# Where fourteen weight loads stand among attention's slots: from slot 3 to 26 instead of from 1 to 26

## The chip, the cores and the metric

The kernel runs on one core of a Trainium2 chip. The metric is the device time of one execution in microseconds (us). The runs are unprofiled; beside them stands one execution that the hardware profiler recorded, from which all views of the profile come. Engines in the text: PE (TensorE matmuls; PEld its weight loads), DVE (VectorE), ACT (ScalarE), POOL (GpSimd), SP (SyncE, which only issues DMAs here).

## The reference: what is computed

Blockwise causal attention, whose result is the input of a mixture-of-experts layer with one expert a token:

- `q`, `k`, `v` are 8 batches x 8 heads x 576 tokens x 64 in float32. Scores are `q k^T / 8`, masked so that a block of 64 tokens sees itself and the blocks before it, then a softmax and the product with `v`.
- The result is laid out as `x`, 8 x 576 rows of 512. `logits = x w_gate` (8 experts), `local_gate = sigmoid(x w_local)`. A token takes its own best expert if it is the first of its batch or its local gate is under 0.5, otherwise the expert of the token before it.
- Each token's output is `p[e] * (relu(x w1[e]) w2[e])`, with `w1` 8 x 512 x 1024 and `w2` 8 x 1024 x 512, and `p` the softmax of the logits.

## The kernel before

**Attention in 32 slots.** A slot is one pair of heads of one batch (`NPAIR = 32`, four slots a batch); the loop is `for i in range(NPAIR)` at line 1045, with `r = i % 4`. The order of instructions on each engine is written out by hand (`tc.manual_schedule()`). Slot `i` does, in this order:

1. `load_qk(i + 2)` (line 787): SP issues the loads of k and q of the pair after next, 256 KB each in 1 KB pieces (line 797), and two small ones (line 802). They go into one staging area, so k of pair `i + 2` can only be issued when POOL has copied k of pair `i + 1` out of it.
2. `behind(i)` (line 1037): `values(i - 1)` on PE (line 920), the additions of the softmax sums on DVE (line 932), and `load_v(i + 1)` on SP (line 813): two v loads of 128 KB in 256-byte pieces (line 819), one a head, and a small one. There are two v buffers, so v of pair `i + 1` is issued when `values(i - 1)` is done with its buffer, and it is read by `values(i + 1)` in slot `i + 2`. In slot 1 alone (`swap`) `behind` comes after the scores.
3. The scores of pair `i` on PE (line 882), their exponentials on ACT (line 892), and POOL's clearing of masked corners (line 869), for which `values(i)` waits.
4. `transposes(i + 1)`: PE transposes k and q of the next pair (line 844), ACT copies them out of PSUM (line 839).
5. `tasks(i)`: for r = 0 and 2 the sums and gates of half a batch (line 696); for r = 1 logits and two tiles of rows of `x` of the batch before; for r = 3 its other three tiles. Each tile of rows is stored to HBM by SP (line 668, 128 KB, the last one 64 KB). In the first batch slots 1 and 3 have no tasks. Beside that, short steps of the routing run on DVE; in slot 4 they make constants on POOL (lines 222 to 246).
6. `arrange(i + 2)` (line 805): POOL copies k and q of the pair after next into the order that the transposes need (line 810, two copies).
7. At the end of some slots, `load_weights` (line 105): POOL issues one DMA that reads 2 MB of float32 weights and writes 1 MB of bf16. Even loads are a `w1` (line 107), odd ones a `w2` (line 111). Which slots these are is what the change touches.

The last two weight loads do not go by that formula: `w1` of expert 7 follows the routing's first half, `w2` of expert 7 stands at slot 30, since their space is scratch and staging until then.

**The experts.** After attention 38 tiles of up to 128 tokens are gathered by expert, multiplied by `w1` (line 994) and `w2` (line 1128) on PE, and scattered to the output (line 1135). Nothing there is touched.

**Queues.** All DMAs issued by SP share one queue on each of the chip's DMA engines (q1 in the profile), all issued by POOL another one (q0). SP issues in order and waits before an issue when the DMA eight issues earlier has not landed.

Of the kernel before, what the change touches and what calls it, by code (L numbers as in the profile page):

```python
# [62 lines left out]
def kernel(  # L63
# [23 lines left out]
    E = moe_w_gate.shape[1]  # L87
# [125 lines left out]
    def row_of_x(x):  # L213
        return x[:, :XH].bitcast(BF16)
# [551 lines left out]
    with tc.tile_pool(name="atn_const", bufs=1) as cst, \  # L766
# [13 lines left out]
        def constants():  # L780
            nc.vector.memset(sel, 0.0)
            nc.vector.memset(sel[:, 16 + E + 1:16 + E + 2], 1.0)
            nc.vector.memset(L[64:, :, :], 0.0)
# [3 lines left out]
        def load_qk(i):  # L787
            if i >= NPAIR:
                return
            b, p = divmod(i, HP)  # L790
            h2 = slice(2 * p, 2 * p + 2)
            tl = ld.tile([P, 2, D], F32, tag="qkl", name="qkl")
            raws[i] = [tl]
            for j, src in enumerate((k, q)):

                m = staged[:, j].rearrange("p (h j d) -> p h j d", h=2, j=4)
                nc.sync.dma_start(
                    out=m.rearrange("p h j d -> p h (j d)"),
                    in_=src[b, h2, :512].rearrange("h (p j) d -> p h (j d)", j=4))
                raws[i].append(m)  # L800
            for j, src in enumerate((k, q)):
                nc.sync.dma_start(out=tl[64 * j:64 * j + 64],
                                  in_=src[b, h2, 512:].rearrange("h s d -> s h d"))

        def arrange(i, copies):
            if i >= NPAIR:
                return
            for j in range(2):
                m = staged[:, 2 + j].rearrange("p (j h d) -> p j h d", j=4, h=2)
                copies[j](m, raws[i][1 + j].rearrange("p h j d -> p j h d"))  # L810
                raws[i][1 + j] = m
# [41 lines left out]
        def transposes(i, copy):  # L853
            if i >= NPAIR:
                return
            ps = psp.tile([P, 2, 512], F32, tag="sc", name="kq")
            for part in range(2):
                turn_part(i, part, ps[:, part])
            back_in_order(i, slice(0, 2), ps, copy)
            turn_tail(i)  # L860
# [10 lines left out]
        def scores(i, u):  # L871
            if i >= NPAIR:
                return
            if u == 0:
                Ss[i] = Sb[i % NSB]
            t = qkTs[i % 2]
            ps = psp.tile([P, 2, 512], F32, tag="sc", name="sc")
            col = 0
            for c, q0, n in UNITS[u]:
                for h in range(2):  # L880
                    r = slice(64 * h, 64 * h + 64)
                    nc.tensor.matmul(ps[:, h, col:col + n], lhsT=t[r, 0, c * P:c * P + P],  # L882
                                     rhs=t[r, 1, q0:q0 + n], start=True, stop=True)
                col += n
            return ps

        def exps(i, u, ps):
            if i >= NPAIR:
                return
            for col, n, c, q0 in EXPS[u]:  # L890
                rows = slice(0, CW[c])
                nc.scalar.activation(exps_at(i, c, q0, n, rows), ps[rows, :, col:col + n],  # L892
                                     func=AF.Exp, scale=scale_attn)
            for c, q0, n in UNITS[u]:
                if q0 == c * P and c < 4:
                    clear(i, c)

        def last_scores(i):
            if i >= NPAIR:
                return  # L900
            t = qkTs[i % 2]
            for h in range(2):
                r = slice(64 * h, 64 * h + 64)

                nc.tensor.matmul(po[:, LAST[h]:LAST[h] + ST],
                                 lhsT=t.rearrange("p a s -> p (a s)")[r, 512:512 + P],
                                 rhs=t[r, 1, 512:], start=True, stop=True)
            for h in range(2):
                nc.scalar.activation(Pc[i % 2][:ST, h, POS[4]:],
                                     po[:ST, LAST[h]:LAST[h] + ST],  # L910
                                     func=AF.Exp, scale=scale_attn)
# [14 lines left out]
        def add_chunks(i):  # L926
            if not 0 <= i < NPAIR:
                return
            for c in range(1, NC):
                n = S - P * c  # L930
                rows = slice(0, CW[c])
                nc.vector.tensor_add(Ss[i][rows, :, P * c:], Ss[i][rows, :, P * c:],  # L932
                                     Pc[i % 2][rows, :, POS[c]:POS[c] + n])
# [44 lines left out]
        def weights_at(w, ev):  # L978
            nc.vector.tensor_copy(w, w1_bf[:, bass.ds(ev, WE)])  # L979
            return w  # L980
# [21 lines left out]
        def expert(ph, j, engines=(mybir.EngineType.PE, mybir.EngineType.DVE)):  # L1002
            return nc.values_load(
                et_i[ph][0:1, j:j + 1], engines=engines, min_val=0,
                max_val=(E - 1) * WE,
                skip_runtime_bounds_check_because="the table is clamped to the last expert")

        def bf(x, n):
            return x.rearrange("p a s -> p (a s)").bitcast(BF16)[:, :n]
# [25 lines left out]
        wload = 0  # L1035

        def behind(i):

            values(i - 1)
            if not swap:  # L1040
                add_chunks(i - 1)
            load_v(i + 1)
            steps.vector(1.4)

        for i in range(NPAIR):
            slot[0] = i
            load_qk(i + 2)


            swap = i == 1  # L1050
            if not swap:
                behind(i)
            if i == NPAIR - 1:

                tiles = [(0, j) for j in range(NS[0])] + [(1, j) for j in range(NS[1])]
                ev = {j: expert(*tiles[j]) for j in range(2)}
                w = weights_at(bf(Pc[0], WE), ev[0])

                free = bf(Sb[(NPAIR - 3) % NSB], 2 * S * 2)[:, -AHEAD * Dm:]
                xTs = {}  # L1060
                for j in range(AHEAD):
                    xTs[j] = free[:, j * Dm:(j + 1) * Dm].rearrange("p (k n) -> p k n", k=KO1)
                    nc.sync.dma_start(out=xTs[j], in_=row_of_x(xgs[j]), transpose=True)
            for u in range(len(UNITS)):
                exps(i, u, scores(i, u))
                if u == 0:
                    last_scores(i)
                    if i == 0:
                        transposes(1, nc.vector.tensor_copy)
                        constants()  # L1070
                        for h in range(2):
                            hs = slice(64 * h, 64 * h + 64)
                            nc.sync.dma_start(
                                out=wg2[hs, :, 16 * h:16 * h + E],
                                in_=moe_w_gate.rearrange("(p h d) e -> h d p e", h=2, d=D)[h])
                            nc.sync.dma_start(
                                out=wg2[hs, :, 16 * h + E:16 * h + E + 1],
                                in_=moe_w_local.rearrange("(p h d) e -> h d p e", h=2, d=D)[h])
            if swap:
                behind(i)  # L1080
            if i:
                transposes(i + 1, nc.scalar.copy)
            if swap:
                add_chunks(i - 1)
            for x in pending.pop(0) if pending else []:
                x()
            steps.tensor()
            steps.vector(2.0)
            for group in tasks(i):
                half.clear()  # L1090
                for out in [x() for x in group]:
                    out()
            slot[0] = i + 0.5
            if i == NPAIR - 1:

                w_next = weights_at(qkT.rearrange("p j a s -> p (j a s)").bitcast(BF16)[:, :WE],
                                    ev[1])
            steps.tensor()
            steps.vector(2.7)
            arrange(i + 2, [nc.gpsimd.tensor_copy] * 2)  # L1100

            if i == 1 + 25 * wload // 13 and wload < 2 * E - 2:
                load_weights(*divmod(wload, 2))
                wload += 1
            if i == NPAIR - 2:

                load_weights(E - 1, 1)
# [13 lines left out]
    with tc.tile_pool(name="ffn_s", bufs=2) as f_p, \  # L1121
# [148 lines left out]
        i = len(tiles) - 1  # L1270
# [31 lines left out]
```

## Time and profile before

| | us |
|---|---|
| median of 3 runs | 445.74 |
| lowest, highest | 445.46, 446.09 |
| the profiled execution | 444.11 |
| its span, first to last instruction | 442.2 |

| engine | busy us | share of the span |
|---|---|---|
| PE | 423.8 | 96% |
| PEld | 309.3 | 70% |
| DVE | 255.1 | 58% |
| ACT | 257.6 | 58% |
| POOL | 185.3 | 42% |

Attention takes the first 282 us or so, the experts the rest. A busy share is a mean over stages with different limits, and PE's counts a matmul that runs at a lower clock as busy for all of its longer time. So the stage is what is read: the chain of work that ended last tells which wait or engine set the time at each place, the timeline which instruction waited for what, and the granted clock (1.0 is full speed) how fast PE was allowed to run there. A DMA's landing time runs from its issue to the last update of its semaphore.

### The profile page before, as it was taken

To read this page: it belongs to the slowest core of one execution; us is meant where nothing else is said; L and a number is where in the kernel's file an instruction comes from. 1 tells how busy PE (TensorE), PEld (TensorE's weight loads), DVE (VectorE), ACT (ScalarE), POOL (GpSimd) and SP (SyncE) were. 2 spreads that over 40 slices of the span, in tenths; PEclk is the share of its full clock that TensorE was granted. 3 is DMA by queue.
4 is the path that set the end of the run, shared out by engine and by line. 5 is a ranking of instruction groups with operands and counts; after the bars stand their busy time and mean duration, and the time that the engine had idled before them with its cause. 6 is when DMAs were issued, how large, how long until landed. Compare 5 with 4: busy or idle time off the path is not lost.

```text
span 442.2 us, 11716 instructions
## 1 busy us (share of the span) xinstructions
PE 423.8 (96%) x4260; PEld 309.3 (70%) x4281; DVE 255.1 (58%) x554; ACT 257.6 (58%) x409; POOL 185.3 (42%) x309
## 2 busy tenths in 40 slices
PE   8997999999999999999999999999799999999995
PEld 6775777677687676776776778657577767767763
DVE  3362454563563467868789976887788433333320
ACT  3763676577567656665677567534354545555552
POOL 2433423223212312123323514315757777767733
PEclk9997999999999999999999999999999999999999
DMA  5598399889799897986989884972847465556441
GB/s 161 138 209 167 92 199 190 187 185 181 182 180 185 181 190 174 191 125 145 183 171 215 156 217 75 188 130 87 167 133 159 114 159 137 147 142 151 134 104 72
DMA packets 113817, 69.65 MB, mean 157 GB/s; under 512 B 77024, under 2 KB 106208, under 8 KB 113761
## 3 DMA queue, kind: packets, MB, share of 16 engines
q1 hardware_dynamic: 96352, 37.94, 37.8%
q0 software_dynamic: 17408, 30.96, 34.9%
q8 instruction: 36, 0.59, 0.6%
q14 instruction: 21, 0.16, 0.1%
HBM read 66.88 MB, written 14.70 MB: 184 GB/s over the span
## 4 chain that ended last, share of the span: by engine, by line
PE 64%; DMA 14%; POOL 8%; issue 7%; ACT 4%; DVE 2%; POOLq 1%; SPq 1%; ACTq 0%; DVEq 0%
PE o L920 19%; PE sc L882 17%; PE trg L696 6%; PE kq L844 6%; DMA xg<-x_rows,idx 6%; PE ps_h L994 5%; POOL xg L653 5%; PE ps_y L1128 4%; DMA v<-in_v_dram 3%; PE trx L710 3%; POOL out_dram L1135 2%; DMA xT<-xg 2%; ACT Pc L892 2%; DMA w_bf<-in_q_dram 1%; DMA w_bf<-in_k_dram 1%
## 5 line engine op out<-in xcount | busy, mean ns | idle before, releaser
L932 DVE TENSOR_TENSOR S<-S,Pc 128x896 f32<-128x896 f32 (+3 forms) x128 | 90.3, 706 | 21.0 <-PE o L920 12.8
L882 PE MATMUL sc<-qkT 64*128 64x288 f32 (+3 forms) x768 | 98.8, 390 | 0.1
L882 PEld LDWEIGHTS sc<-qkT 64*128 64x128 f32 x768 | 68.8, 187 | 14.0 <-ACT qkT L839 0.5
L979 DVE COPY w1c<-w_bf 128x4096 bf16 x36 | 44.5, 1236 | 57.3 <-PE ps_h L994 53.7
L994 PEld LDWEIGHTS <-w1c 128*128 128x128 bf16 x1152 | 67.0, 98 | 13.0 <-issue 4.1
L994 PE MATMUL ps_h<-xT,w1c 128*128 128x128 bf16 x1088 | 66.3, 219 | 4.2 <-DMA xT<-xg 2.9
L924 ACT COPY oT<-o 128x576 f32<-128x576 f32 x32 | 20.5, 639 | 84.8 <-PE o L920 73.9
L1128 PE MATMUL ps_y<-w_bf,hT 128*128 x283 | 67.6, 379 | 1.1
L653 POOL DMA_INDIRECT xg<-x_rows,idx x38 | 56.1, 1477 | 23.1 <-issue 10.2
L839 ACT COPY qkT<-kq 128x1024 f32<-128x1024 f32 (+1 forms) x31 | 64.7, 2087 | 1.8 <-PE kq L844 1.6
L892 ACT ACTIVATE Pc<-sc 128x448 f32<-128x448 f32 (+1 forms) x96 | 63.9, 707 | 0.0
L810 POOL COPY w_bf<-w_bf 128x512 f32<-128x512 f32 x61 | 44.2, 745 | 44.1 <-DMA w_bf<-in_k_dram 20.0
L997 ACT ACTIVATE hT<-ps_h 128x512 bf16<-128x512 f32 x76 | 45.3, 597 | 29.4 <-PE ps_h L994 26.1
L920 PE MATMUL o<-Pc,v 128*64 128x320 f32 (+2 forms) x512 | 59.8, 373 | 0.0
L1135 POOL DMA_INDIRECT out_dram<-y,idx x38 | 44.1, 1160 | 35.3 <-ACT y L1133 20.2
L920 PEld LDWEIGHTS o<-Pc,v 128*64 128x64 f32 x512 | 36.9, 140 | 23.5 <-issue 0.2
L1133 ACT ACTIVATE y<-ps_y,xg 128x512 f32<-128x512 f32 x38 | 26.1, 688 | 45.1 <-PE ps_y L1128 43.2
L892 ACT ACTIVATE S<-sc 128x576 f32<-128x576 f32 x64 | 41.6, 650 | 15.6 <-PE sc L882 15.6
L1128 PEld LDWEIGHTS <-hT 128*128 128x128 bf16 x304 | 28.2, 98 | 27.7 <-issue 0.5
L869 POOL MEMSET Pc<- 64x128 f32 x96 | 17.5, 200 | 63.4 <-ACT Pc L892 59.4
L920 PE MATMUL o<-S,v 128*64 128x256 f32 (+1 forms) x256 | 39.7, 425 | 3.4 <-DMA v<-in_v_dram 2.5
L869 POOL MEMSET S<- 64x128 f32 x32 | 6.4, 200 | 86.5 <-ACT S L892 85.3
(287 smaller groups left out, 424.8 us busy)
## 6 DMA issues: line engine op xcount, KB each, us to landing
w_bf<-in_moe_w_dram POOLq DMA_DIRECT2D x16, 1024.0 KB, 10.4
w_bf<-in_k_dram SPq DMA_DIRECT2D x32, 256.0 KB, 3.6
w_bf<-in_q_dram SPq DMA_DIRECT2D x32, 256.0 KB, 4.5
v<-in_v_dram SPq DMA_DIRECT2D x64, 128.0 KB, 3.0
x_rows<-xg SPq DMA_DIRECT2D x24, 128.0 KB, 5.1
qkl<-in_k_dram SPq DMA_DIRECT2D x32, 32.0 KB, 3.7
qkl<-in_q_dram SPq DMA_DIRECT2D x32, 32.0 KB, 7.7
vl<-in_v_dram SPq DMA_DIRECT2D x32, 32.0 KB, 2.7
```

Of the source, the lines that this page charges most:

```text
L653: nc.gpsimd.indirect_dma_start(out=x, out_offset=None, in_=x_dram[:rows], in_offset=bass.IndirectOffsetOnAxis(ap=row_of(ph, j), axis=0), b ...
L810: copies[j](m, raws[i][1 + j].rearrange("p h j d -> p j h d"))
L839: copy(qkTs[i % 2][:, parts, :512].rearrange("p a (s j) -> p a j s", j=4), ps.rearrange("p a (j s) -> p a j s", j=4))
L882: nc.tensor.matmul(ps[:, h, col:col + n], lhsT=t[r, 0, c * P:c * P + P], rhs=t[r, 1, q0:q0 + n], start=True, stop=True)
L892: nc.scalar.activation(exps_at(i, c, q0, n, rows), ps[rows, :, col:col + n], func=AF.Exp, scale=scale_attn)
L920: nc.tensor.matmul(po[64 * h:64 * h + 64, VO + q0:VO + q0 + n], lhsT=vv, rhs=exps_at(i, c, q0, n, slice(0, P))[:, h, :], start=(c == 0), s ...
L932: nc.vector.tensor_add(Ss[i][rows, :, P * c:], Ss[i][rows, :, P * c:], Pc[i % 2][rows, :, POS[c]:POS[c] + n])
L979: nc.vector.tensor_copy(w, w1_bf[:, bass.ds(ev, WE)])
L994: nc.tensor.matmul(ps[:, fo, :], lhsT=w[:, ko * F + f0:ko * F + f0 + P], rhs=xT[:, ko, :], start=(ko == 0), stop=(ko == KO1 - 1))
L997: nc.scalar.activation(hT[:, half * (FO // 2):(half + 1) * (FO // 2), :], ps, func=AF.Relu)
L1128: nc.tensor.matmul(ps, lhsT=hT[:, fo, :], rhs=w2_bf[:, bass.ds(ev + fo * Dm, Dm)], start=(fo == 0), stop=(fo == FO - 1))
L1135: st = nc.gpsimd.indirect_dma_start(out=out_flat, out_offset=bass.IndirectOffsetOnAxis(ap=row_of(ph, j), axis=0), in_=y, in_offset=None, b ...
```

## The change

One condition in the slot loop is different. `wload` counts the loads from 0 to 13; load `2e` is `w1` of expert `e`, load `2e + 1` its `w2`.

```
-            if i == 1 + 25 * wload // 13 and wload < 2 * E - 2:
+            if i == 3 + 23 * wload // 13 and wload < 2 * E - 2:
                 load_weights(*divmod(wload, 2))
                 wload += 1
```

| load | 0 | 1 | 2 | 3 | 4 | 5 | 6 | 7 | 8 | 9 | 10 | 11 | 12 | 13 |
|---|---|---|---|---|---|---|---|---|---|---|---|---|---|---|
| slot before | 1 | 2 | 4 | 6 | 8 | 10 | 12 | 14 | 16 | 18 | 20 | 22 | 24 | 26 |
| slot after | 3 | 4 | 6 | 8 | 10 | 11 | 13 | 15 | 17 | 18 | 20 | 22 | 24 | 26 |

The place within a slot (behind `arrange`), the loads themselves and their order are the same.

## The prediction

> **What bounds the kernel now.** I read the page first, then the chain that ended last in order of time, then the timeline of the first 50 us, then the DMA queues and the landing times of single loads. The page gives the span and, among the DMA issues, what a weight load and a v load cost from issue to landing (last column, us, median).
>
> ```profile
> span 442.2 us, 11716 instructions
> ```
> ```profile
> w_bf<-in_moe_w_dram POOLq DMA_DIRECT2D x16, 1024.0 KB, 10.4
> ...
> v<-in_v_dram SPq DMA_DIRECT2D x64, 128.0 KB, 3.0
> ```
>
> The chain (start, length, what) shows PE work through attention, a slot every 8.3 to 8.8 us, with one large exception.
>
> ```profile
> 24.43 14.40 DMA v<-in_v_dram
> 38.88 5.59 PE o L920 x23
> ...
> 50.51 2.85 PE o L920 x28
> ...
> 67.79 2.85 PE o L920 x28
> ...
> 119.20 2.85 PE o L920 x28
> ...
> 125.07 1.02 PE kq L844 x8
> ```
>
> The reader is to see two things. A v load that usually lands in 3.0 us is in the chain for 14.40 us. And the matmuls of `values` (L920) that follow it take 5.59 us for 23 pieces, where any other slot takes 2.85 us for all 28. The timeline (start, length, engine, line; in brackets the idle time before, and who ended it) shows what surrounds that load:
>
> ```profile
> 21.94 0.96 POOL L107 DMA_DIRECT2D w_bf<-in_moe_w_dram  x1
> ...
> 23.79 1.15 SPq L819 DMA_DIRECT2D v<-in_v_dram  x2
> ...
> 28.24 0.94 POOL L111 DMA_DIRECT2D w_bf<-in_moe_w_dram  x1
> ...
> 35.48 0.35 POOL L869 MEMSET Pc<- 64x128 f32 x2 [1.88 <-ACT Pc L892]
> ...
> 35.72 0.62 PE L920 MATMUL o<-S,v 128*64 128x256 f32 x2 [0.43 <-POOL Pc L869]
> ...
> 38.88 1.65 PE L920 MATMUL o<-S,v 128*64 128x256 f32 x5 [2.54 <-DMA v<-in_v_dram]
> ```
>
> Weight load 0 is issued at 21.94 (end of slot 1), v(3) at 23.79 (slot 2), weight load 1 at 28.24 (end of slot 2), only 6.3 us after load 0, where one such load needs 10.4 us to land. `values(3)` in slot 4 starts at 35.72, does the first two pieces with head 0, and then waits 2.54 us for the second half of v(3). What the engines did in 24 to 40 us (q0 is POOL's queue: weights alone here), and what PE's clock did in the stage from slot 3's scores to slot 4's, and in the next one (us, then busy time and instruction count of PE, PEld, DVE, ACT, POOL, then the granted clock, the DMA share, GB/s):
>
> ```profile
> q0 software_dynamic: 1560, 2.09, 76.8%
> ```
> ```profile
> 31.10:44.40 13.30, 10.33 (x67) 7.97 (x65) 4.57 (x8) 5.66 (x9) 3.85 (x11) 0.76 0.87 178
> 44.40:53.30 8.90, 8.90 (x91) 6.07 (x90) 2.94 (x11) 5.79 (x9) 4.24 (x18) 0.98 0.27 71
> ```
>
> Two weight loads back to back held 76.8% of the DMA engines' time just when v(3) had to get through, and the wait brought the granted clock of that stage down to 0.76. So PE bounds attention everywhere, and in this one place DMA does.
>
> [...]
>
> **The change part by part.** Nothing is added or removed: the same fourteen DMA issues on POOL's queue, the same tiles, the same order of loads. Before, they stand at the ends of slots 1, 2, 4, 6, 8, 10, 12, 14, 16, 18, 20, 22, 24, 26. By the new formula they stand at 3, 4, 6, 8, 10, 11, 13, 15, 17, 18, 20, 22, 24, 26. From load 9 (slot 18) on nothing moves.
>
> *Slots 1 and 2 lose their loads.* With both gone, v(3) has only k, q and its own pieces on the engines. I take the usual 3.0 us: landed by about 28, needed at 35.72. The loss that goes: `values(3)` now lasts from 35.72 to 38.88 + 5.59 = 44.47, that is 8.75 us; with v there it lasts 2.85 us. Gain 5.9 us. Of it 2.54 us are the wait, and 3.36 us are matmuls at the lower clock. What is late next in that slot is POOL's clear at 35.48, which already sets the start at 35.72 and so is in the sum.
>
> *Slots 3 and 4 get loads 0 and 1.* POOL's issue takes 0.96 us (row at 21.94). In slot 3 it stands behind the clear that ends at 35.83 and two copies of `arrange(5)`; in slot 4 behind constants and `arrange(6)`:
>
> ```profile
> 46.49 0.20 POOL L869 MEMSET S<- 64x128 f32 x1 [2.27 <-ACT S L892]
> ...
> 51.53 2.03 POOL L810 COPY w_bf<-w_bf 128x512 f32<-128x512 f32 x2
> 53.51 0.78 POOL L107 DMA_DIRECT2D w_bf<-in_moe_w_dram  x1
> ```
>
> Behind the issue in POOL's queue in slot 4 are the constants and the clear at 46.49; POOL was idle 2.27 us before that, which hides 0.96 us. So it costs nothing; without that cover it would cost 0.96 us once. Load 0 should go out at about 35.83 + 1.2 = 37.1 (two copies take 1.17, row at 109.74 below), and load 1 where load 2 stood, 53.51 less 5.9 = 47.6. That is 10.5 us apart instead of 6.3, and a load lands in 10.4: the pair no longer piles up.
>
> *All other shifted loads* (slots 4 to 17) change places or kinds (L107 or L111). Their price is what they may do to k, q and v of the next slots. The nearest rows:
>
> ```profile
> 102.10 0.88 POOL L111 DMA_DIRECT2D w_bf<-in_moe_w_dram  x1
> ...
> 109.74 1.17 POOL L810 COPY w_bf<-w_bf 128x512 f32<-128x512 f32 x2
> ```
> ```profile
> 105.34 1.32 SPq L819 DMA_DIRECT2D v<-in_v_dram  x1
> ```
> ```profile
> DMA to landing us min/median/max: 10.8/10.8/10.8
> ```
> ```profile
> 84.81 0.75 POOL L107 DMA_DIRECT2D w_bf<-in_moe_w_dram  x1
> ```
> ```profile
> 84.90 1.63 SPq L797 DMA_DIRECT2D w_bf<-in_q_dram  x1
> ```
> ```profile
> DMA to landing us min/median/max: 10.7/10.7/10.7
> ```
>
> Two landing rows, each of the one issue above it: v(12), issued at 105.34, lands at 116.14, 14.0 us after its weight load, and is needed at 119.20. q(11), issued at 84.90, lands at 95.6, 10.8 us after its weight load. I check three places. (a) v(6), needed at 67.79, 14.3 us after the load at 53.51, which in the new kernel is of the L111 kind: 14.3 against 14.0, a margin of 0.3 us, the thinnest. (b) Slots 10 and 11: load 5 would leave after the copies at 109.74, at 110.9, 8.8 us after the one at 102.10. v(12) has 119.20 - 102.10 = 17.1 us. In the bad pair of slots 1 and 2, only 6.3 us apart, v(3) was there 38.88 - 21.94 = 16.9 us after the first load, so even that would just do. (c) k and q of pair 14 meet that load 5: 110.9 + 10.8 = 121.7 for q(14), plus a copy of about 0.6, against 125.07 when PE transposes it; 2.8 us of margin. Slots 15, 17 and 18 repeat (b) and (c). The cost of all these lies between 0 and 5.9 us a place (slot 4's loss, the only price the trace has); a gain is excluded, since PE is busy through such a slot (8.90 of 8.90 us in the stage after the stall) and can't be made to wait less. I take 0, as every margin worked out is positive.
>
> *SP's queue* issues the same DMAs in the same order. It is held back where weights fill the engines (the 1.32 us issue at 105.34), so it gains in slots 2 and 3 and loses in 12, 14 and 16, hidden by the margins above.
>
> **Sum.** The profiled execution took 444.11 us: 442.2 of span and 1.9 around it; less 5.9 it is 438.2. It is 1.6 us under the median of the runs, 445.74. I subtract from the median: 445.74 - 5.9 = **439.8 us**.
>
> **Rivals.**
>
> *A thin margin breaks, in one place.* Most likely v(6) in slot 6, margin 0.3 us. If it lands 1 us later than v(12) did, PE waits 0.7 us; with the lower clock behind it, up to 3.36 us more: 440.5 to 443.9, middle about 442. For it: the L111 kind and 0.3 us. Against: load 1 is no longer pushed by a load 6.3 us ahead of it. [...]
>
> *Only the wait goes, not the low clock.* If the 0.76 came from the light slot 3 itself and not from the wait, `values(3)` would still take about 5.6 us and only 2.54 us would go: 443.2. Against it: PE works from 35.72 on without a break once v is there.
>
> *Slower.* The loads now fall at the ends of odd slots, 11 and 15 among them, where three stores of x rows go out on SP's queue just ahead of k and q. If these push q(14) and q(18) past their transposes by more than the 2.8 us of (c), PE waits in slots 13 and 17, each as dear as slot 4 was: 445.74 - 5.9 + 2 x 5.9 = 451.6. One such place alone makes it even at 445.7; from the second on it is slower. Against: 2.8 us is more than SP's three stores of 128 KB or less can take at the stage's rate of 178 GB/s (2.2 us).
>
> *The load of v(3) is slow by itself,* so that nothing changes: 445.7. Against it stand the 3.0 us median of 64 such loads.
>
> **How the numbers follow.** A change is seen on this kernel from about 0.2% on (0.9 us). Full gain 0.68 (439.8), one broken margin 0.17 (442), only the wait 0.06 (443.2), slower 0.06 (451.6), even 0.03. Faster: 0.68 + 0.17 + 0.06 = 0.91; same 0.03; slower 0.06. Range: below, the 1.6 us that the unprofiled runs are longer may sit in the same place, 438.2, and the runs differ by 0.3 either way: 438.0. Above it takes in the broken margin and the lost wait: 443.3.
>
> **What would show it.** Right: no v row of over 4 us in the chain before 40 us; `values(3)` starts near 35.7 and ends near 38.6; slot 3's stage is about 7.5 us at a clock of 1.0; the weight issues at about 37 and 47.6; everything from slot 5 on is the old timeline less 5.9. Wrong: PE waits on v near 61.9 (v(6)), on POOL's copies near 119 (q(14)), or a stage in slots 4 to 18 with a clock under 0.95. I am wrong in size if the unprofiled runs do not hold the stall that the profile shows.

## The result and the profile after

The changed kernel is not faster but a little slower. Its median is 448.10 us over 18 executions (445.85 to 451.46) against 446.18 us over 18 of the kernel before, timed beside them (443.67 to 453.74). The ratio is 1.005 with a 95% interval of 1.0029 to 1.0071. That ratio leaves out executions more than 1.5% above the fastest of their kernel, which by this rule are four of before's 18 (451.05 to 453.74 us); the medians of all executions stand at 1.004. I had forecast 439.8 us.

And yet, in the recorded execution, the stall of slot 4 is gone as forecast. The chain of the changed kernel (start, length, what) has no v load near 35 us, and `values(3)` takes 2.93 us. What it has instead stands at 193 us:

```profile
span 446.2 us, 11716 instructions
```
```profile
31.00 1.09 PE sc L882 x8
33.46 1.87 issue
35.58 2.93 PE o L920 x28
38.51 1.06 PE sc L882 x8
...
189.92 1.23 SPq L668
191.82 1.37 SPq L668
193.29 5.10 DMA w_bf<-in_k_dram
199.21 1.27 PE kq L844 x8
```

Two stages, first of the changed kernel and then the second one of the kernel before (us, then busy time and count of PE, PEld, DVE, ACT, POOL, then the granted clock, DMA share, GB/s): slot 3, and slots 21 to 23 together.

```profile
30.94:38.44 7.50, 7.07 (x69) 5.53 (x66) 3.06 (x6) 5.82 (x9) 3.37 (x10) 1.00 0.32 73
...
186.12:214.69 28.57, 26.65 (x254) 19.64 (x252) 19.70 (x57) 17.42 (x28) 7.92 (x21) 1.00 0.86 157
```
```profile
192.26:219.23 26.97, 26.47 (x255) 19.72 (x251) 19.42 (x56) 17.29 (x28) 7.59 (x19) 1.00 0.86 163
```

Slot 3 went from 13.3 to 7.50 us (with slot 4's 8.90 to 8.75 that is the forecast 5.9), and the lead of 6.1 us holds up to slot 21 (186.12 against 192.26). In slots 21 to 23, where PE is busy for about as long (26.65 and 26.47 us), 1.6 us are lost. The timeline of the changed kernel shows how (POOL, SP and PE; idle time before in brackets, and who ended it):

```profile
36.87 0.95 POOL L107 DMA_DIRECT2D w_bf<-in_moe_w_dram  x1
...
47.40 0.95 POOL L111 DMA_DIRECT2D w_bf<-in_moe_w_dram  x1
...
156.72 0.75 POOL L107 DMA_DIRECT2D w_bf<-in_moe_w_dram  x1
...
167.93 1.85 POOL L810 COPY w_bf<-w_bf 128x512 f32<-128x512 f32 x2 [4.42 <-PE o L920]
169.73 0.88 POOL L111 DMA_DIRECT2D w_bf<-in_moe_w_dram  x1
...
174.57 3.72 SPq L668 DMA_DIRECT2D x_rows<-xg  x3
...
183.94 1.70 SPq L819 DMA_DIRECT2D v<-in_v_dram  x2
...
186.42 6.77 SPq L668 DMA_DIRECT2D x_rows<-factors  x8
193.29 0.53 SPq L797 DMA_DIRECT2D w_bf<-in_k_dram  x1
...
198.54 1.23 POOL L810 COPY w_bf<-w_bf 128x512 f32<-128x512 f32 x2 [7.67 <-DMA w_bf<-in_k_dram]
...
199.21 1.27 PE L844 MATMUL kq<-id_f,w_bf 128*128 128x128 f32 x8 [1.48 <-POOL w_bf L810]
```

The same places of the kernel before, whose clock of events runs 6.14 us later at slot 21:

```profile
170.93 0.89 POOL L111 DMA_DIRECT2D w_bf<-in_moe_w_dram  x1
...
180.85 1.68 SPq L668 DMA_DIRECT2D x_rows<-xg  x3
...
189.71 6.76 SPq L668 DMA_DIRECT2D x_rows<-factors  x8
196.57 0.53 SPq L797 DMA_DIRECT2D w_bf<-in_k_dram  x1
...
201.87 2.10 POOL L810 COPY w_bf<-w_bf 128x512 f32<-128x512 f32 x2 [4.86 <-DMA w_bf<-in_k_dram]
```

Read them in order of time. Load 8 leaves at the end of slot 17 (156.72), not 16, and k of pair 20 lands beside it, so that POOL's copies start only at 167.93, after 4.42 us of idling. (The row puts that wait down to PE; in r2_after below, the same kernel, the landing is on record: k of pair 20 is issued at 158.79 and lands 8.7 us later, and the copies start at 167.67.) Load 9 stands behind these copies and leaves at 169.73; before it left at 170.93, which is 164.8 on this axis, so it is 4.9 us later in the slot. SP's queue then falls behind: three stores take 3.72 us instead of 1.68, and the eight stores of the routing's `factors` (6.8 us of SP in either kernel) start 0.3 us after slot 21's scores instead of 2.55 us before. k of pair 23 stands behind them. It is issued 7.2 us after slot 21's scores instead of 4.3, POOL idles 7.67 us for it, and PE waits 1.48 us for POOL's copy: a loss in slot 22, from a load that moved in slot 16.

The rest of the difference, in this one recording, is in the experts: 168.2 us from slot 31's scores to the end, where the recording of before had 160.5. Whether the change does that was the first question for the experiments.

### The profile page after: what moved, and what is told of

It is laid out like the page before. It is cut to its first block, busy times and chain, and to the rows that moved or that the text cites. A ratio compares the mean times of both kernels' runs of the same rounds, so it can differ in the third digit from the quotient of the medians.

```text
span 446.2 us, 11716 instructions
## 1 busy us (share of the span) xinstructions
PE 421.6 (95%) x4260; PEld 308.0 (69%) x4281; DVE 255.8 (57%) x554; ACT 254.9 (57%) x409; POOL 179.3 (40%) x309
## 4 chain that ended last, share of the span: by engine, by line
PE 59%; issue 15%; DMA 11%; POOL 7%; DVE 3%; ACT 2%; SPq 2%; POOLq 1%; DVEq 0%; ACTq 0%
PE o L920 17%; PE sc L882 16%; DMA xg<-x_rows,idx 6%; PE kq L844 6%; PE trg L696 6%; PE ps_h L994 4%; PE ps_y L1128 4%; POOL xg L653 4%; DMA w_bf<-in_k_dram 4%; PE trx L710 3%; POOL out_dram L1135 2%; SPq L668 2%; ACT qkT L839 1%; PE trl L718 1%; PE o L905 1%
## 5 line engine op out<-in xcount | busy, mean ns | idle before, releaser
L932 DVE TENSOR_TENSOR S<-S,Pc 128x896 f32<-128x896 f32 (+3 forms) x128 | 93.0, 727 | 16.5 <-PE o L920 8.4
L994 PE MATMUL ps_h<-xT,w1c 128*128 128x128 bf16 x1088 | 67.9, 219 | 10.1 <-ACT hT L997 5.4
L1135 POOL DMA_INDIRECT out_dram<-y,idx x38 | 51.6, 1357 | 52.2 <-ACT y L1133 33.2
L810 POOL COPY w_bf<-w_bf 128x512 f32<-128x512 f32 x61 | 45.8, 772 | 64.2 <-DMA w_bf<-in_k_dram 36.0
L920 PE MATMUL o<-Pc,v 128*64 128x320 f32 (+2 forms) x512 | 57.5, 366 | 0.0
L920 PEld LDWEIGHTS o<-Pc,v 128*64 128x64 f32 x512 | 36.0, 137 | 22.7
L653 POOL DMA_INDIRECT xg<-x_rows,idx x38 | 41.0, 1080 | 21.3 <-issue 10.5
L1128 PEld LDWEIGHTS <-hT 128*128 128x128 bf16 x304 | 28.2, 98 | 27.7 <-issue 0.5
L850 DVE COPY qkT<-o 128x128 f32<-128x128 f32 x32 | 9.3, 290 | 55.9 <-PE o L848 55.9
L920 PE MATMUL o<-S,v 128*64 128x256 f32 (+1 forms) x256 | 38.3, 418 | 1.0 <-POOL Pc L869 0.4
```

What stands on the lines that cost most here:

```text
L653: nc.gpsimd.indirect_dma_start(out=x, out_offset=None, in_=x_dram[:rows], in_offset=bass.IndirectOffsetOnAxis(ap=row_of(ph, j), axis=0), b ...
L920: nc.tensor.matmul(po[64 * h:64 * h + 64, VO + q0:VO + q0 + n], lhsT=vv, rhs=exps_at(i, c, q0, n, slice(0, P))[:, h, :], start=(c == 0), s ...
L994: nc.tensor.matmul(ps[:, fo, :], lhsT=w[:, ko * F + f0:ko * F + f0 + P], rhs=xT[:, ko, :], start=(ko == 0), stop=(ko == KO1 - 1))
L1128: nc.tensor.matmul(ps, lhsT=hT[:, fo, :], rhs=w2_bf[:, bass.ds(ev + fo * Dm, Dm)], start=(fo == 0), stop=(fo == FO - 1))
L1135: st = nc.gpsimd.indirect_dma_start(out=out_flat, out_offset=bass.IndirectOffsetOnAxis(ap=row_of(ph, j), axis=0), in_=y, in_offset=None, b ...
```

## The experiments

The theories, in words. For the experts: the slower rhythm comes with the change, or it is chance. For slot 22: the pair of loads in slots 17 and 18 alone makes the loss, or something else in the shift does. For the gain that is missing in the times: the stall of slot 4 is in every execution of the kernel before, or only in some. All stage times below are differences of the first scores matmuls of the slots in the recorded execution; "experts" is from slot 31's scores to the end. Ratios are against the kernel before in the same session, that is, among runs timed together. The row called 'before' and the row called 'after' are the first pair of recordings, whose ratio is the result's.

| run | loads differ from before in | slot 3 | slots 21-23 | experts | ratio of times, 95% interval |
|---|---|---|---|---|---|
| before | - | 13.33 | 26.97 | 160.5 | - |
| r1_before | - | 11.89 | 26.96 | 159.4 | 1.0004 [0.9970, 1.0037] |
| r9_before | - | 10.74 | 27.02 | 159.6 | 1.0029 [0.9993, 1.0065] |
| r13, r14, r15_before | - | 7.50, 7.50, 7.50 | 26.98, 26.98, 27.01 | 167.2, 167.7, 168.1 | one execution each |
| after | the change | 7.50 | 28.57 | 168.2 | 1.005 [1.0029, 1.0071] |
| r2_after | the change | 7.50 | 29.19 | 159.1 | 1.0025 [0.9992, 1.0058] |
| r10_after | the change | 7.50 | 29.33 | 159.4 | 1.0082 [1.0052, 1.0113] |
| r16_after | the change | 7.50 | 29.89 | 171.2 | one execution |
| r3_load1_late | load 1 in 3 | 7.50 | 27.02 | 160.8 | 0.9981 [0.9956, 1.0006] |
| r7_load1_late | load 1 in 3 | 7.50 | 27.38 | 159.7 | 1.0005 [0.9977, 1.0032] |
| r11_load1_late | load 1 in 3 | 7.50 | 27.12 | 161.4 | 1.0007 [0.9973, 1.0041] |
| r5_load8_at_17 | load 8 in 17 | 7.50 | 30.06 | 161.0 | 1.001 [0.9972, 1.0047] |
| r4_load8_at_16 | the change, load 8 in 16 | 7.50 | 27.02 | 160.2 | 1.0025 [0.9995, 1.0055] |
| r8_load8_at_16 | the change, load 8 in 16 | 7.50 | 27.39 | 163.9 | 1.003 [1.0004, 1.0056] |
| r6_both_in_1 | loads 0 and 1 both in 1 | 11.50 | 27.02 | 160.1 | 1.0103 [1.0076, 1.0131] |
| r12_3_4_5_6 | loads 0 to 3 in 3, 4, 5, 6 | 7.50 | 27.09 | 160.7 | 1.0109 [1.0024, 1.0193] |

**Both kernels again, unchanged.**

> The kernel before once more, for a second profile. Theory R (rhythm): the 7.7 us that the changed kernel lost behind attention belong to a slower rhythm of the experts' stage (7.8 us per two tiles instead of 7.0), into which the changed timing of attention leads; then this run shows the stall of 5.9 us in slot 4 and the fast rhythm, about 160 us from the start of slot 31 to the end, and a span of about 442. Theory C (chance): the rhythm differs from execution to execution whatever the kernel; then this run may show the slow one, with a span near 450.

> The changed kernel once more. Theory R: no stall in slot 4, attention at slot 31 about 3.7 us earlier than in the kernel before, and again the slow rhythm with about 168 us from slot 31 to the end: span near 446, ratio to before about 1.005. Theory C: the rhythm is as likely to be fast, about 160 us behind slot 31 and a span near 438.

The changed kernel runs its experts in 159.1 us here, so their slow rhythm isn't the change's work. Its loss in slot 22 is there again (29.19 us for slots 21 to 23).

**Load 8 alone.** The pair of loads in 17 and 18 is put back in the changed kernel, and made alone in the kernel before:

```
-            if i == 3 + 23 * wload // 13 and wload < 2 * E - 2:
+            if wload < 2 * E - 2 and i == [3, 4, 6, 8, 10, 11, 13, 15, 16, 18, 20, 22, 24, 26][wload]:
...
-            if i == 1 + 25 * wload // 13 and wload < 2 * E - 2:
+            while wload < 2 * E - 2 and i == [1, 2, 4, 6, 8, 10, 12, 14, 17, 18, 20, 22, 24, 26][wload]:
```

> The changed kernel with load 8 back from slot 17 to slot 16. If the pair of loads in slots 17 and 18 is what pushes SP's queue so far back that k(23) is late in slot 22 (1.5 us of waiting there, 2.4 us lost between slots 22 and 27), slot 31 starts about 2.4 us earlier than in the changed kernel, near 275.6. If that loss comes from elsewhere, slot 31 starts at 278 as in the changed kernel. The experts' stage is open, as in the run before.

> The changed kernel with load 8 back in slot 16 once more, for a closer interval. Theory P expects slot 21 to slot 24 to last 27.0 us and a timed ratio to the kernel before of 0.997 to 0.999, as with load 1 alone moved; theory S, or a loss in the other shifted loads 5 to 7, expects 1.002 to 1.005.

> The kernel before with load 8 alone moved, from slot 16 to slot 17, so that loads 8 and 9 stand in neighbouring slots. Theory P (pair): this pair alone makes k(20) late, so POOL issues load 9 some 5 us later, SP's queue falls behind, k(23) lands late and PE waits 1.5 us in slot 22; the stretch from slot 21 to slot 24 lasts 29.2 us instead of 27.0, and the timed ratio is 1.004 to 1.006. Theory S (sum of all shifts): it takes the later loads 5 to 7 too; then the stretch lasts 27.0 us and the ratio is 1.000.

Slots 21 to 23, with load 8 put back in the changed kernel (r4) and then with load 8 alone moved in the kernel before (r5):

```profile
188.35:215.37 27.02, 26.47 (x255) 19.68 (x252) 19.49 (x57) 17.36 (x28) 7.25 (x18) 1.00 0.86 160
```
```profile
186.06:216.12 30.06, 26.89 (x256) 19.68 (x252) 19.29 (x55) 17.44 (x28) 6.74 (x19) 1.00 0.85 151
```

One part alone makes the loss in this stage, and undoing it takes the loss away (27.39 in r8). Over all recordings the five with loads in 17 and 18 take 28.57 to 30.06 us here, the other thirteen 26.96 to 27.39. So the pair costs 1.6 to 3.1 us in every recorded execution. The other shifted loads cost nothing that the recordings show: slots 5 to 17 take the same time to 0.01 us in all of them, but for slot 6 of r12.

The times do not show as much. With the pair alone r5 stands at 1.001, where 1.004 to 1.006 was expected; without the pair r4 and r8 stand at 1.0025 and 1.003, where theory P had put r8 under 1 and theory S at 1.002 to 1.005. The kernel before, timed against itself, gave 1.0004 and 1.0029 (r1, r9), so these sessions can't tell a ratio of 1.003 from 1. Both recordings, r4's and r8's, lost some 1.9 us at the very start, where the clock was granted at 11.5 us (5.0 to 9.3 us in the others), and slot 4 starts at 40.4 us instead of 38.4. Why that was so in both is open.

r5 brought a second thing, not expected: it has loads 0 and 1 where the kernel before has them, and no stall.

**Load 1 alone, and both loads together.**

```
-            if i == 1 + 25 * wload // 13 and wload < 2 * E - 2:
+            if wload < 2 * E - 2 and i == [1, 3, 4, 6, 8, 10, 12, 14, 16, 18, 20, 22, 24, 26][wload]:
...
+            while wload < 2 * E - 2 and i == [1, 1, 4, 6, 8, 10, 12, 14, 16, 18, 20, 22, 24, 26][wload]:
```

> The kernel before with load 1 alone moved, from slot 2 to slot 3; loads 2 to 13 where they were. The stall theory (two loads 6.3 us apart starve v(3)) expects the stall of 5.9 us in slot 4 gone and no new loss in slots 12 to 26, so slot 31 starts about 6 us earlier than in the kernel before (275.7 against 281.7). For the end, theory R has no fixed number: 436 if the fast rhythm stays, 444 if any shift of attention brings the slow one. Theory C: 436 or 444 by chance.

> Load 1 from slot 2 to slot 3 once more, for a closer interval. Theory I expects: no execution with a clock under 0.995, none over 1.5% above the lowest, and a median 0.2 to 0.5% under that of the kernel before, since only the executions with the stall gain. If the stall were in all executions of the kernel before, the ratio would be 0.986.

> Only load 1 moved, from slot 2 to 3; all others as before. No stall in slot 4, slot 22 at 9.1 to 9.6 us. If the stall is in one execution in five, the median is that of before's undisturbed executions and the ratio 0.996 to 1.000; if the pair of loads in 17 and 18 is not what the changed kernel loses by, it is no faster than the changed kernel.

> The kernel before with load 1 moved from slot 2 to slot 1, right behind load 0. Theory I (the stall in slot 4 is real but comes only in some executions, since v(3) lands close to its deadline): with the loads 1 us apart v(3) passes both at once or is late always, so the stall is there in all executions or in none. If in all: the timed ratio is about 1.010 to 1.014, and the granted clock lies under 0.995 in most executions. If in none: ratio 0.997 to 1.000 and clocks from 0.996 on. A stall in a minority again, as in the kernel before (clock under 0.9955 in 8 of its 35 runs), would say that the spacing of the two loads is not what sets it.

Moving load 1 by one slot takes the stall away in all three recordings, so the mechanism of the forecast holds. But the times hardly move: three ratios whose intervals lie between 0.9956 and 1.0041, and by the medians of all executions 0.9972, 0.9994 and 1.0004. A stall of 3.2 to 5.9 us in every execution would have to give 0.987 to 0.993, and none of these reaches there. The smaller gain that r7 and r11 allowed for did not show either (1.0005 and 1.0007). Both loads in slot 1 on the other hand make the stall, with the ratio at 1.0103, about 4.5 us. Slot 3 of that kernel:

```profile
31.13:42.63 11.50, 9.37 (x69) 7.38 (x65) 3.93 (x7) 5.65 (x9) 3.69 (x11) 0.85 1.03 209
```

**How often the stall is there.** The kernel before was recorded four times more, and both kernels and the load 1 variant timed once more.

> The kernel before, unchanged. Theory 'the stall comes and goes': about one unprofiled execution in five lies some 4 to 5 us above the rest, and those are the ones with a granted clock under 0.996; the profiled one shows slot 3 either at about 7.5 us (no wait on v(3)) or at 11.5 to 13.5 us. Rival 'always there in a profile': slot 3 takes 11.5 us or more a third time.

> The changed kernel, unchanged. No execution with the stall, but slot 22 at 10.5 to 11.5 us instead of 9.1, PE waiting 1.4 to 1.7 us on POOL's copy of k(23). If the typical execution of the kernel before has no stall, the changed one loses what slot 22 costs, 1.6 to 2.2 us: ratio 1.002 to 1.006 on the medians. If the stall is in most executions: ratio 0.990 to 0.995.

> The kernel before, unchanged, one more recorded execution. Theory 'the stall is in a minority of executions' (the times): one in four of these four looks shows slot 3 at over 10 us, and those without it take some 3 to 6 us less from the first instruction to slot 5 (47.2 instead of 50.4 to 53.3). Rival 'in nearly every recorded one' (the profiles so far: 3 of 3): all four show 10.7 us or more.

> As for the look before it: the kernel before, slot 3 at 7.5 us (minority theory) or at 10.7 us or more (in nearly every recorded one).

> As for the two looks before it. If the wait on v(3) is there, theory 'the low clock depends on when the wait falls' expects 0, 3.41 or 6.83 us at half clock behind a wait of about the same 2.3 to 2.6 us.

> The changed kernel, one more recorded execution: slot 3 at 7.5 us, slots 21 to 27 together 64.5 us or more, where kernels without a pair of loads in 17 and 18 take 62.0 to 63.8.

Slot 3 of r9_before and of r14_before, the same program:

```profile
30.88:41.62 10.74, 7.68 (x70) 6.06 (x66) 3.06 (x6) 5.66 (x9) 1.68 (x6) 1.00 1.05 204
```
```profile
30.86:38.36 7.50, 7.07 (x70) 5.53 (x66) 3.06 (x6) 5.86 (x9) 3.23 (x11) 1.00 1.20 222
```

Of six recordings of the kernel before, three hold the stall (13.33, 11.89, 10.74 us) and three, all of one session, do not. That is more than the one in four that I expected, and less than "nearly every recorded one". Without the stall the kernel before reaches slot 4 at 38.30 to 38.75 us, which is where the changed kernel does (38.14 to 38.47): there is nothing to gain in such an execution. r16_after was recorded in the same session as those three and again has the loss: 29.89 us against 26.98 to 27.01 in slots 21 to 23. r10_after has it too (29.33), and its ratio, 1.0082, is above the 1.002 to 1.006 expected.

What lets v(3) through in one execution and not in the next? The issues of loads 0 and 1, first of r9_before (stall), then of r14_before (none):

```profile
21.75 0.96 POOL L107 DMA_DIRECT2D w_bf<-in_moe_w_dram  x1
...
28.05 0.94 POOL L111 DMA_DIRECT2D w_bf<-in_moe_w_dram  x1
```
```profile
20.87 0.96 POOL L107 DMA_DIRECT2D w_bf<-in_moe_w_dram  x1
...
28.04 0.94 POOL L111 DMA_DIRECT2D w_bf<-in_moe_w_dram  x1
```

The two loads are 6.3 us apart in the three recordings with the stall, and 7.2, 7.3 and 8.3 us in the three without it. It is load 0 that is late: it leaves at 21.75 to 21.94 us with the stall and at 20.72 to 21.13 without, while load 1 leaves at 28.0 to 28.2 us in five of the six. But r5, with 6.3 us, has no stall. Between the end of load 0's traffic and the start of load 1's, near 30 to 32 us, SP's queue (q1) has most of the DMA engines' time. The view of the DMA queues for just these 2 us (packets, MB, share of 16 engines; a packet counts in the window in which it starts, so a share can pass 100%) of the first recording, r9_before, r5 and r14_before, in this order:

```profile
q1 hardware_dynamic: 1240, 0.45, 88.8%
q0 software_dynamic: 62, 0.09, 25.4%
```
```profile
q1 hardware_dynamic: 1021, 0.34, 72.3%
q0 software_dynamic: 88, 0.15, 40.5%
```
```profile
q1 hardware_dynamic: 1271, 0.45, 89.4%
...
q0 software_dynamic: 57, 0.08, 25.1%
```
```profile
q1 hardware_dynamic: 1275, 0.56, 111.8%
...
q0 software_dynamic: 10, 0.01, 2.9%
```

More passes in r14_before (0.56 MB), which has no stall, than in r9_before (0.34 MB), where the second half of v(3) waits for load 1 as well and lands at 38.73 us. In r5 it is down at 32.93 us, 8.73 us after its issue. Yet the first recording, with the longest stall, moved the same 0.45 MB as r5, which has none. So the spacing of the two loads matters, as both variants show (both loads in one slot make the stall, load 1 one slot later takes it away), but what decides at 6.3 us is open: the traffic through the gap doesn't tell the two apart.

**Loads one slot apart elsewhere.**

```
+            if wload < 2 * E - 2 and i == [3, 4, 5, 6, 8, 10, 12, 14, 16, 18, 20, 22, 24, 26][wload]:
```

> Loads 0 to 3 at the ends of slots 3, 4, 5, 6, the others as before (8, 10, ... 26). It has the first part of the change (nothing in slots 1 and 2) without the pair in 17 and 18. If four loads about 9 us apart harm nothing: slot 3 at 7.5 us, slot 22 at 9.1 us, ratio 0.996 to 1.000. If loads one slot apart cost wherever they stand, as those in 17 and 18 do, 1.5 to 2.5 us go in slots 6 to 10 and the ratio is 1.002 to 1.006.

The second expectation holds in kind: neighbouring loads cost PE a wait here too. In size it is passed, by 3.3 us against 1.5 to 2.5 and by a ratio of 1.0109 against 1.002 to 1.006 (its interval is wide). v(6) lands 14.74 us after its issue, and slot 6 takes 12.02 us where it takes 8.75 elsewhere. The chain of that kernel:

```profile
51.13 14.74 DMA v<-in_v_dram
65.87 0.04 issue
65.91 2.92 PE o L920 x23
```

This is the stall of v(3) again, three slots later, with load 1 at 48.4 us and load 2 at 54.1 us, 5.7 us apart. Of the loads in neighbouring slots, those in 1 and 2 (in some executions), 4 and 5, and 17 and 18 cost PE a wait; those in 3 and 4, 10.5 us apart, cost none, and those in 10 and 11 left a margin of 0.2 us.

**The experts' rhythm.** From slot 31's scores to the end, in r9_before and r14_before:

```profile
279.22:438.84 159.62, 148.32 (x1657) 107.97 (x1674) 79.12 (x155) 76.89 (x126) 95.78 (x76) 0.99 0.56 133
```
```profile
276.23:443.88 167.65, 149.91 (x1657) 108.32 (x1674) 79.80 (x156) 74.50 (x126) 88.28 (x76) 1.00 0.52 127
```

The kernel before shows both, 8 us apart, with the same work. All four recordings of the last session (r13 to r16) have the slower rhythm; the twelve of r1 to r12 take 159.1 to 161.4 us but for r8 (163.9), whose experts hold 3.41 us at half clock from 315.28 us on. The chip is not what makes it: r1 to r4 ran on the same chip as r13 to r16. What does is open.

## Why the prediction was wrong

**The step that failed** is "I subtract from the median: 445.74 - 5.9". The stall was in the recorded execution (and in three of six recordings of this kernel) and, by the three ratios of load 1 alone, not in most of the timed ones. I had checked the recorded time against the median, found 1.6 us between them, and took them for the same thing. They differed twice, and the two nearly cancelled: the recording had the stall (5.9 us more) and the fast experts (160.5 us, where the sessions near 446 us have 167 to 168: 7.1 us less on the mean of r13 to r15). 444.11 - 5.9 + 7.1 = 445.3, and r13 to r15, without a stall, took 445.7 to 445.9 us. That fits a median without a stall to take away; the timed executions of the first session left no stages in which to see it. The prediction's last sentence named this condition, but gave it no chance of its own.

**The second step that failed** is "I take 0, as every margin worked out is positive". The measured cost of "slots 15, 17 and 18 repeat (b) and (c)" is 1.6 to 3.1 us, and it falls in slot 22. I checked each load against the k, q and v of the next two slots. The lateness didn't stop there: it went into POOL's issue of load 9, from there into SP's queue, and met the eight stores of `factors`, which neither (b) nor (c) had. "*SP's queue* ... loses in 12, 14 and 16, hidden by the margins above" is the same mistake. These 1.6 to 3.1 us, 0.4 to 0.7%, are of the size of the whole measured loss (0.5%). That they are that loss is not shown, since the times of r4 and r8, without the pair, are not under those of the kernel before.

**Point by point.**
- Stall of slot 4 and its price: right for the executions that hold it. Slot 4 began at 38.44 us instead of 44.40, 5.96 us earlier for the 5.9 forecast; issues at 36.87 and 47.40 for 37.1 and 47.6; slot 3 at 7.50 us and clock 1.00. That 5.9 us is the largest of three prices, though: slot 3 lost 5.8, 4.4 and 3.2 us in the three recordings with the stall, with 6.83, 3.41 and 0 us at half clock.
- (a) v(6), "the thinnest" with 0.3 us: it held, and no recorded execution of the changed kernel waits there. r12, with load 2 one slot earlier, shows what it costs when v(6) is late: 3.3 us in slot 6.
- (c) q(14) with 2.8 us: far too large. POOL's second copy began at 118.12 and PE's transposes at 118.90, so 0.2 us or so were left. It just held, and its margin was carried on to slots 17 and 18, where nothing of the kind was left.

```profile
118.12 0.61 POOL L810 COPY w_bf<-w_bf 128x512 f32<-128x512 f32 x1 [1.26 <-PE sc L882]
```
```profile
118.90 1.09 PE L844 MATMUL kq<-id_f,w_bf 128*128 128x128 f32 x8
```

- The rival "slower" had the right path (SP's stores ahead of k and q, which come too late for their transposes) at the wrong place: k(23) in slot 22, not q(14) and q(18), behind the eight stores of `factors`, and without a lower clock behind the wait (1.00 in the stage above). Its argument against itself, 2.2 us for three stores of x rows, did not hold: three such stores took SP 3.72 us at 174.57. It asked for two such places to outweigh the gain; without the gain one is enough.
- Stalls and the clock: with a wait of 2.54 us the clock came down in the first recording, with one of 2.63 us in the same place it did not (r9_before, 1.00 in slot 3), while with 1.70 us it did in r6 (0.85).

```profile
38.10 1.36 PE L920 MATMUL o<-S,v 128*64 128x256 f32 x5 [1.70 <-DMA v<-in_v_dram]
```
```profile
38.77 0.91 PE L920 MATMUL o<-S,v 128*64 128x256 f32 x5 [2.63 <-DMA v<-in_v_dram]
```

In the first recording the clock stood at full for 30.72 us, at half for 6.83 us (37.89 to 44.72 us) and at full again for 395.95 us; r6 has it at half for 3.41 us, from 38.43 us on. In the 3.41 us before the low clock (34.48 to 37.89 us) PE was busy for 1.43 us in the first recording. Here are the 3.42 us before the low clock in r6, with PE busy for 1.29 us, and that low clock, then two stretches of the same length over which the wait of r9_before was spread, with PE busy for 2.19 and 1.57 us and the clock at 1.00:

```profile
35.01:38.43 3.42, 1.29 (x10) 0.55 (x9) 0.29 (x1) 2.32 (x2) 0.34 (x2) 1.00 1.17 277
38.43:41.84 3.41, 3.41 (x20) 2.89 (x18) 1.61 (x2) 0.00 (x0) 2.39 (x7) 0.50 0.73 152
```
```profile
33.52:36.93 3.41, 2.19 (x17) 1.30 (x13) 0.29 (x1) 3.41 (x4) 0.35 (x2) 1.00 1.20 224
36.93:40.34 3.41, 1.57 (x15) 1.39 (x17) 0.25 (x1) 0.15 (x1) 0.00 (x0) 1.00 1.06 197
```

So the length of a wait does not tell by itself whether the clock comes down. What decides it is not shown.

No version beats the kernel before by more than the measurement tells. Load 1 alone moved is level with it, and none of its three recordings has the stall.

## What to carry to other kernels

A stall in one recording is not yet a stall in the median: record the kernel again, and compare stage by stage, before a gain is subtracted, above all where recording and median agree only in the sum. When a transfer is moved later, follow the lateness through every queue behind it until a slot has caught up, not only to the next reader; here a load moved from slot 16 to 17 cost PE its wait in slot 22, behind a burst of small stores that had been hidden.

## What the runs showed of the hardware

- With loads 0 and 1 issued 6.3 us apart in the same slots, v(3) landed 8.7 us after its issue in one recording (r5) and 14.5 us in another (r9_before). The first recording of the kernel before, with the longest stall, and r5 both moved 0.45 MB through SP's queue in the 2 us between the two loads.
- A wait of PE on v(3) of 1.70 us came with 3.41 us at half clock (r6), one of 2.54 us with 6.83 us of it (the first recording of the kernel before), and one of 2.63 us with none (r9_before).
- The experts' part took 159 to 161 us in twelve of the 18 recordings, 163.9 us in one and 167 to 171 us in five, among them both kernels.
